# Value products ahead of a score tile behind a tanh, tanhs kept out of the last product steps, and a reordered tail in a fused attention and GEGLU block

## The chip, the cores and the metric

The kernel runs on one core of one Trainium2 chip. The metric is the device time of one execution in microseconds (us). The kernel before takes 1223.26 us, the median of 3 runs (1223.11 to 1223.34). Five engines work side by side: TensorE (PE, with its weight loads as PEld), VectorE (DVE), ScalarE (ACT), GpSimd (POOL) and SyncE (SP, which issues the DMAs).

## What is computed

A transformer block in bfloat16 on x of shape 1 x 2048 x 512, with 32 heads of 16 and a feed-forward width of 1792:

```python
q, k, v = split(layernorm(x) @ wqkv)
scores = einsum("bhqd,bhkd->bhqk", q, k) * Dh ** -0.5
h = x + merge(einsum("bhqk,bhkd->bhqd", softmax(scores), v)) @ wo
n = layernorm(h)
out = h + (gelu(n @ w_gate) * (n @ w_up)) @ w_down
```

The gelu is the tanh form. The scores are 32 x 2048 x 2048 values, each computed twice by this kernel: once for the row maximum, once (transposed) for the exp.

## The kernel before

**Units and ticks.** The queries are cut into 8 groups of 256, the heads into 8 slots of 4. A unit is one group and one slot (later ones: one half group and two slots); there are 64. The main loop (L1642) counts ticks, 16 to a unit. In each tick a first pass works on one unit and a second pass on the unit 24 ticks behind it:

- First pass: two matmuls (L883, `p1_pair`) write two 128 x 512 score tiles, and one reduction on DVE (L898) takes the row maxima of both. One tick of each of 14 units (JOINT) is saved by a difference trick on DVE (L895), with an `item_diff` that computes a difference beforehand.
- Second pass: two score tiles, transposed (L974, `p2_tile`), of which each gets its own exp on ACT (L1003) into a ring of 34 probability tiles.

Each score tile takes one of eight PSUM banks: four serve the first pass as a ring of two pairs, four (4 to 7) the second pass, handed out by `Banks` in the order in which they come free. A tile waits for the exp that last read its bank.

**The dense stream.** All other TensorE work is cut into pieces of about half a tick: generator functions that yield after some matmuls (`Dense`, L540). It holds one of the four banks while an item runs. Per tick one piece is issued, behind the two score tiles; without one, filler matmuls (L1618, `dummy`) take its place. The items are

- `item_pv` (L1006): the value products of one unit, probabilities times values, in four steps at ticks 15, 16, 17 and 18 of its second pass, which are ticks 7, 8, 9 and 10 of a unit by the loop's count. Behind the last step ACT copies the result out (OB, L727).
- the projections, the output projection (`item_oproj`, L1188), gate and up products of the feed-forward part (L1378, and L1323 in its half-group form), and down products (L1422).

**Gelu.** In the main stage the gelu is a polynomial on POOL (L1303 to L1305), a tanh on ACT (L1293) and two products on POOL (L1301, L1302), then a product with the up half (L1414 or L1359). When the tanh is recorded is decided by `later` in `gelu_chain` (L1285): it defers itself tick by tick while a model of ACT's backlog (`act_lag`) is too high or ticks are "tight".

**Order.** `Plan` records each engine's instructions in program order and derives the semaphore waits. The waits of a tick's first two matmuls and of its first score tile are gathered on the first of them (`group_begin`, `group_end`). Engines run their lists strictly in order. `deferred` calls run at the end of a tick, so what `later` records stands on ACT behind both exps of its tick.

**The end.** After the last first-pass tick, the second pass goes on alone: four tiles (two pairs) each even tick, one exp for each pair (L991), DVE takes over copies, and the dense stream fills PE. On an even tick `alone` keeps the cost of the dense piece, and on the odd tick behind it at least FILL_2 - alone is filled (L1737). There the last group's first half goes through `item_oprojA`, `item_hnA` (L1241), which transposes the normalized rows, and the raw gate and up products (GA, UA).

**The tail** (`tail_b`, L1549) computes the last half group: gelu of GA (L1517), GUT = GA * UA in four parts (`raw_mult`, L1521; part 0 on POOL, 1 to 3 on DVE), the output projection of the last rows (L1461 to L1567), their normalization (L1570 to L1577), transposes (`tail_hnT`, L1500) and copies (L1505, L1507), the seed of the last sums (`end_h`, L1541), gate, up and down products of the last 128 rows (L1323, L1546), while the down products of the rows before them (`down_mm`, L1422) are placed in between. `fill(n)` issues dense pieces, or fillers, worth n.

Of the kernel before, what the change touches and what calls it, by code (L numbers as in the profile page):

```python
# [215 lines left out]
NFC = F // 128  # L216
# [15 lines left out]
FILL_2 = 5  # L232
FILL_A = 2
# [15 lines left out]
def bass_sequential_preLN__mha_block__geglu_ffn__prompt_kernel(nc, A_x, A_wqkv, A_wo, B_x, B_w_gate, B_w_up, B_w_down, out):  # L249
    dbg = None  # L250
    with ExitStack() as es:
# [99 lines left out]
        GL = NG - 1  # L351
# [188 lines left out]
        class Dense:  # L540
            def __init__(self):
                self.prio = []
                self.ready = []
                self.extra = []
                self.gen = None
                self.under = None
                self.bank = None
                self.banks = [7, 3, 4, 5]
                self.rr = 0
                self.pause = 0  # L550
                self.single = False
                self.done = 0
                self.now = 0
# [6 lines left out]
            def _start(self, item):  # L560
                genfn, a, est, nb = item
                self.cur = genfn
                if self.single:
                    self.bank = banks.take()
                else:
                    self.bank = self.banks[self.rr % len(self.banks)]
                    self.rr += 1
                self.gen = genfn(self.bank, *a)
# [137 lines left out]

        act_lag = [0.0]
        def act_more(cost):
            act_lag[0] += cost
# [296 lines left out]
        def item_pv(b, ui, ps=(0, 1, 2, 3)):  # L1006
# [3 lines left out]
            for p in ps:  # L1010
                while not force[0] and dense.now < P2_START + 16 * ui + pt_t[p]:
                    yield ("wait", 1)
                for m in (2 * p, 2 * p + 1):
                    n, c0, s_ = (2, 0, slot) if ui < UB else (4, 128 * (m // 4), slot + m // 4)
                    qn = 512 // n
                    for i in range(n):
                        kt = 2 * m + i if ui < UB else 4 * (m % 4) + i
                        for g in range(4):
                            pi = pt_of[(ui, m, g)]
                            P.op("pe", lambda e, g=g, kt=kt, pi=pi, i=i, s_=s_, c0=c0, qn=qn: e.matmul(pbank[32 * g:32 * g + 17, b, c0:c0 + qn], VA[:, kt, 4 * s_ + g, :],  # L1020
                                                                                                      PTt(pi)[:, qn * i:qn * i + qn], start=(kt == 0), stop=(kt == NT - 1), tile_position=(0, 32 * g)),
                                 reads=[("V", kt), "VA_ones", ("PT", pi)], writes=[("pb", b)], sig=(g == 3 and i == n - 1))
                    for g in range(4):
                        pt_busy.discard(pt_of.pop((ui, m, g)))
                if p != ps[-1]:
                    yield 2
# [214 lines left out]
        def item_hnA(b):  # L1241
# [5 lines left out]
            defer(1, add_raw)  # L1247
            return 1
            yield
# [30 lines left out]
        def gelu_chain(par, dE, w=512):  # L1280
# [4 lines left out]
            def later(n):  # L1285
                if not force[0] and tight():
                    defer(1, lambda: later(n))
                    return
                if not force[0] and (act_lag[0] + (0.48 if dense.gen is not None and dense.cur in (item_gate, item_up, item_gate_h, item_up_h) else 0) > LAG_TH + SLOPE * n or poly_end[par] > TICK * dense.now + POLY):
                    defer(1, lambda: later(n + 1))  # L1290
                    return
                act_more(0.54 if w == 512 else 0.32)
                P.op("act", lambda e: e.activation(out=ts_, in_=ts_, func=ACT.Tanh, scale=GC), reads=[("th", par)], writes=[("th", par)])  # L1293
                defer(1, second)
# [254 lines left out]
        def tail_b():  # L1549
# [10 lines left out]
            while not a_done[0]:  # L1560
# [3 lines left out]
            in_bank(tail_onT)  # L1564
            raw_mult(1, "dve")
            fill(2)
# [8 lines left out]
            P.op("pool", lambda e: e.tensor_tensor(out=rstd2[:, tt], in0=rstd2[:, tt], in1=nhalf[:, 0:1], op=ALU.pow), reads=[("rstd2", t1), "nhalf"], writes=[("rstd2", t1)])  # L1575
            raw_mult(2, "dve")
            P.op("dve", lambda e: e.tensor_scalar(out=hn_sb[:, 1, :], in0=g_h(GL, 1), scalar1=mv2[:, t1, 0:1], scalar2=rstd2[:, tt], op0=ALU.subtract, op1=ALU.mult),  # L1577
                 reads=[("h", 1, 1), ("mv2", t1), ("rstd2", t1)], writes=[("OH", 1)])
            down_h(0, GL, 0)
            for fc in range(8):  # L1580
                down_mm(0, GL, 0, fc)
            fill(FILL_A)
            tail_hnT(2, (0, 1), "act")
            tail_hnT(3, (2, 3), "dve")
            raw_mult(3, "dve")
            for fc in chunks(2):
                down_mm(0, GL, 0, fc)
            while dense.busy():
# [5 lines left out]
            for t in range(NTL):  # L1594
                tail_gate(gb[2 * t % 5], t)
                tail_up(gb[(2 * t + 1) % 5], t)
                if t == 0:
                    for fc in chunks(3):
                        down_mm(0, GL, 0, fc)
# [42 lines left out]
        while True:  # L1642
# [37 lines left out]
            else:  # L1680
                t1 = p1_pair(tick // 16, tick % 16, gp1) if p1_ok else []
                if doubles[0]:
                    p1_next.append(p1_pair((tick + 1) // 16, (tick + 1) % 16, 1 - gp1))
            t2l = [next_tile()] if p2_ok and p1_ok else []
            P.group_end("pe")
            if p2_ok and p1_ok:
                behind[0] -= 1
                t2l.append(next_tile())
                if more:
# [36 lines left out]
            else:  # L1726
                cost = dense.piece()
                if cost and not p2_started:
# [63 lines left out]
```

## Time and profile before

| | |
|---|---|
| median of the runs | 1223.26 us |
| the profiled execution | 1223.57 us |
| its span, first to last instruction | 1221.5 us |
| granted TensorE clock | 1.000 |
| busy: PE, DVE, ACT, POOL | 1130.1, 1181.4, 1190.9, 840.0 us |
| reductions (L898) | 996, 1134.8 us busy |
| exps (L1003) | 2000, of 710 to 719 ns on average |
| tanhs (L1293) | 50, 42.9 us busy |
| value product matmuls (L1020) | 126.0, 51.2 and 41.8 us in three groups |
| fillers (L1618) | 771, 235.7 us busy |

Busy time is the time in which at least one instruction of an engine is under way. Consecutive instructions on ACT and DVE overlap at their ends, so a row's mean duration is longer than the distance from one start to the next. Rows of the timeline give the start, the duration, engine, line, operation, out<-in with shapes, and a count when like instructions are merged; in square brackets stands the idle time before, with what ended it. In the rows of `waits` stand the total, the number of waits, and the longest.

### The profile page before, as it was taken

The numbers are of one execution on the slowest core, as the hardware profiler recorded it, in microseconds if no ns is written. First come the engines' busy times: TensorE is split into PE (matmuls) and PEld (weight loads), VectorE is DVE, ScalarE is ACT, GpSimd is POOL, SyncE is SP. The second block draws the span as 40 slices with busy tenths as digits, with TensorE's granted clock in tenths as the row PEclk, the third lists the DMA queues.
The fourth block names the chain that finished last, engine by engine and source line by source line (L and its number), as shares of the span: only waits on it lengthen the run. The fifth ranks groups of instructions, "written<-read, shape, count | busy, mean of one in ns | idle before, by whom it ended". The sixth has DMA issues, their size and how long they took to land.

```text
span 1221.5 us, 36085 instructions
## 1 busy us (share of the span) xinstructions
PE 1130.1 (93%) x14842; PEld 476.2 (39%) x14842; DVE 1181.4 (97%) x1125; ACT 1190.9 (97%) x2422; POOL 840.0 (69%) x1772
## 2 busy tenths in 40 slices
PE   7999998899999999999999999999999999999998
PEld 3233332233333333333332333333334455554556
DVE  8999999999999999999999999999999999999973
ACT  7899999999999999999999999999999999999995
POOL 7567684756776586756868487774777687856771
PEclk9999999999999999999999999999999999999999
DMA  5111104300010000110001000100001100010000
GB/s 153 28 33 28 29 24 136 92 8 11 8 28 21 12 11 8 25 23 12 11 22 15 23 8 10 25 21 15 8 8 29 26 18 16 9 27 15 18 17 18
DMA packets 69651, 32.02 MB, mean 26 GB/s; under 512 B 54768, under 2 KB 68464, under 8 KB 69488
## 3 DMA queue, kind: packets, MB, share of 16 engines
q1 hardware_dynamic: 69488, 29.71, 10.0%
q8 instruction: 118, 1.93, 0.6%
q14 instruction: 45, 0.37, 0.1%
HBM read 11.80 MB, written 2.10 MB: 11 GB/s over the span
## 4 chain that ended last, share of the span: by engine, by line
ACT 55%; DVE 34%; PE 9%; issue 1%; POOL 0%; POOLq 0%; DVEq 0%
DVE PM L898 34%; ACT PTM L1003 31%; ACT PTG L1003 10%; ACT PTE L1003 5%; PE pbank L1422 2%; ACT th_sb L1293 2%; ACT g_sb L727 2%; ACT u_sb L727 2%; PE pbank L974 1%; PE pbank L1323 1%; PE pbank L883 1%; ACT OB L727 1%; PE pbank L456 1%; PE pbank L1618 1%; DVE OA L895 1%
## 5 line engine op out<-in xcount | busy, mean ns | idle before, releaser
L898 DVE TENSOR_REDUCE PM<-pbank 128x2 f32<-128x1024 f32 x996 | 1134.8, 1213 | 8.5 <-PE pbank L974 3.8
L1003 ACT ACTIVATE PTM<-pbank 128x512 bf16<-128x512 f32 x1357 | 733.4, 718 | 4.1 <-PE pbank L974 0.6
L974 PE MATMUL pbank<-QT,KT 32*128 32x256 bf16 (+1 forms) x5120 | 506.0, 250 | 14.4 <-ACT PTM L1003 7.9
L883 PE MATMUL pbank<-KT,QT 32*128 32x512 bf16 x2020 | 388.5, 384 | 24.9 <-DVE PM L898 10.2
L1618 PE MATMUL pbank<-ones_bf,ident 128*128 128x512 bf16 x771 | 235.7, 384 | 29.2 <-ACT PTM L1003 4.7
L883 PEld LDWEIGHTS pbank<-KT,QT 32*128 32x128 bf16 x2020 | 97.4, 91 | 350.8 <-DVE PM L898 130.8
L974 PEld LDWEIGHTS pbank<-QT,KT 32*128 32x128 bf16 x5120 | 205.5, 92 | 69.3 <-ACT PTM L1003 40.1
L1003 ACT ACTIVATE PTG<-pbank 128x512 bf16<-128x512 f32 x407 | 225.0, 710 | 0.8 <-PE pbank L974 0.4
L1003 ACT ACTIVATE PTE<-pbank 128x512 bf16<-128x512 f32 x236 | 140.2, 719 | 0.8 <-PE pbank L974 0.5
L1020 PE MATMUL pbank<-PTM,VA 128*17 128x256 bf16 (+1 forms) x3470 | 126.0, 252 | 1.8 <-ACT PTM L991 0.4
L1061 POOL TENSOR_TENSOR LINV<-OBT,negone 128x8 f32<-128x8 bf16 x63 | 105.1, 1669 | 5.7 <-DMA OBT<-OB 5.4
L1618 PEld LDWEIGHTS pbank<-ones_bf,ident 128*128 128x128 bf16 x771 | 45.1, 97 | 132.1 <-ACT PTM L1003 83.8
L1303 POOL TENSOR_TENSOR th_sb<-g_sb 128x512 f32<-128x512 f32 (+1 forms) x50 | 51.2, 1023 | 62.9 <-ACT g_sb L727 62.9
L1020 PEld LDWEIGHTS pbank<-PTM,VA 128*17 128x17 bf16 x3470 | 67.0, 90 | 40.5 <-issue 21.7
L1302 POOL TENSOR_TENSOR th_sb<-th_sb,g_sb 128x512 f32<-128x512 f32 (+1 forms) x50 | 62.4, 1249 | 4.0
L953 POOL TENSOR_TENSOR QT<-QT,STG 128x256 bf16<-128x256 bf16 x64 | 42.8, 668 | 31.3 <-DMA STG<-ST 30.7
L1305 POOL TENSOR_TENSOR th_sb<-th_sb,g_sb 128x512 f32<-128x512 f32 (+1 forms) x50 | 62.3, 1246 | 1.7
L1301 POOL TENSOR_SCALAR th_sb<-th_sb 128x512 f32<-128x512 f32 (+1 forms) x50 | 30.5, 611 | 40.9 <-ACT th_sb L1293 40.8
L1422 PE MATMUL pbank<-wd_sb,GUT 128*128 128x512 bf16 x210 | 57.8, 382 | 0.9 <-POOL GUT L1521 0.3
L798 POOL TENSOR_SCALAR QT<-QKS,qmask 128x512 bf16<-128x512 bf16 x30 | 46.9, 1569 | 13.4 <-ACT QKS L727 12.7
L1378 PE MATMUL pbank<-hnT_l,wg_sb 128*128 128x256 bf16 x336 | 51.2, 275 | 3.3 <-ACT PTM L1003 0.7
L1414 POOL TENSOR_TENSOR GUT<-th_sb,u_sb 128x512 bf16<-128x512 f32 x42 | 53.3, 1268 | 1.3
(197 smaller groups left out, 1210.2 us busy)
## 6 DMA issues: line engine op xcount, KB each, us to landing
QKS<-QKS SPq DMA_DIRECT2D x27, 112.0 KB, 2.1
x_sb<-in_A_x_dram SPq DMA_DIRECT2D x4, 512.0 KB, 5.7
xres<-in_A_x_dram SPq DMA_DIRECT2D x16, 128.0 KB, 2.3
out_dram<-out_sb SPq DMA_DIRECT2D x15, 128.0 KB, 1.7
wg_sb<-in_B_w_gate_dram SPq DMA_DIRECT2D x4, 448.0 KB, 4.2
wu_sb<-in_B_w_up_dram SPq DMA_DIRECT2D x4, 448.0 KB, 3.9
wd_sb<-in_B_w_down_dram SPq DMA_DIRECT2D x3, 512.0 KB, 4.4
STG<-ST SPq DMA_TRANSPOSE x64, 2.3
```

What stands on the lines that cost most here:

```text
L727: P.op("act", lambda e: e.activation(out=o_ap, in_=i_ap, func=ACT.Copy, **kw), reads=reads, writes=writes, extra_deps=extra)
L883: P.op("pe", lambda e, g=g, b=b: e.matmul(pbank[:, b, :], QT[32 * g:32 * g + 32, c, slot, 128 * qt:128 * qt + 128], KT[32 * g:32 * g + 32, ...
L898: P.op("dve", lambda e: e.tensor_reduce(out=PM[:, par, qt, kc, g:g + 2], in_=pbank[:, b:b + 2, :], axis=AX.X, op=ALU.max), reads=[("pb", b ...
L974: P.op("pe", lambda e, kt=kt, i=i: e.matmul(pbank[:, b, qn * i:qn * i + qn], KT[32 * g:32 * g + 32, slot, 128 * kt:128 * kt + 128], QT[32 ...
L1003: P.op("act", lambda e, b=b, pi=pi: e.activation(out=PTt(pi), in_=pbank[:, b, :], func=ACT.Exp), reads=[("pb", b)], writes=[("PT", pi)], e ...
L1020: P.op("pe", lambda e, g=g, kt=kt, pi=pi, i=i, s_=s_, c0=c0, qn=qn: e.matmul(pbank[32 * g:32 * g + 17, b, c0:c0 + qn], VA[:, kt, 4 * s_ + ...
L1061: P.op("pool", lambda e: e.tensor_tensor(out=li, in0=o4[:, :, :, 16], in1=negone[:, 0:4 * nq].rearrange("p (q h) -> p q h", q=nq), op=ALU. ...
L1302: o(1.27, lambda e: e.tensor_tensor(out=ts_, in0=ts_, in1=gs, op=ALU.mult), [("th", par), ("g", par)])], then=done)
L1305: o(1.27, lambda e: e.tensor_tensor(out=ts_, in0=ts_, in1=gs, op=ALU.mult), [("th", par), ("g", par)])], then=poly_done)
L1414: P.op("pool", lambda e: e.tensor_tensor(out=o_ap, in0=shp(ts_), in1=shp(us), op=ALU.mult), reads=[("th", par), ("u", par)], writes=o_keys ...
L1422: P.op("pe", lambda e: e.matmul(pbank[:, b, :], GUT[:, fc, 128 * k:128 * k + 128], wd_sb[:, fc, :], start=first, stop=last), reads=[("GUT" ...
L1618: P.op("pe", lambda e: e.matmul(pbank[:, b, :], ident[:], ones_bf[:, 0:512], start=True, stop=True), reads=["ident", "ones_bf"], writes=[( ...
```

## The change

Four things:

1. `dense.plain` is set while `item_pv` stands behind its first or second step. In the main loop, in a tick exactly two behind the one that recorded a tanh (`th_step`), with `dense.plain` set and no third tile, the dense piece (the second or third step of the value products) is issued between the two score tiles instead of behind them.
2. `later` doesn't record a tanh in ticks 9 and 10 of a unit while the value products are the running item; it tries again a tick later.
3. `item_hnA` returns FILL_2 (5) as its cost instead of 1, so that the odd tick behind it is not filled.
4. In the tail, GUT parts 1 and 2 are computed one place later on DVE (part 1 behind the statistics, part 2 behind the copies of the transposes), the FILL_A pieces come ahead of the seed `down_h` instead of behind eight down products, and down products 8 to 11, which stood behind the transposes, are issued with 12 and 13 behind the first gate and up products.

```diff
@@ Dense._start
                 self.cur = genfn
+                self.plain = False
@@ item_pv
+                dense.plain = p != ps[-1] and p + 1 != ps[-1]
                 if p != ps[-1]:
                     yield 2
@@ item_hnA
-            return 1
+            return FILL_2
@@ gelu_chain, later
-                if not force[0] and tight():
+                if not force[0] and (tight() or dense.gen is not None and dense.cur is item_pv and dense.now % 16 in (9, 10)):
                     defer(1, lambda: later(n))
                     return
...
                 act_more(0.54 if w == 512 else 0.32)
+                th_step[0] = dense.now
@@ tail_b
             in_bank(tail_onT)
-            raw_mult(1, "dve")
             fill(2)
...
-            raw_mult(2, "dve")
+            raw_mult(1, "dve")
             P.op("dve", lambda e: e.tensor_scalar(out=hn_sb[:, 1, :], ...
+            fill(FILL_A)
             down_h(0, GL, 0)
             for fc in range(8):
                 down_mm(0, GL, 0, fc)
-            fill(FILL_A)
             tail_hnT(2, (0, 1), "act")
             tail_hnT(3, (2, 3), "dve")
+            raw_mult(2, "dve")
             raw_mult(3, "dve")
-            for fc in chunks(2):
-                down_mm(0, GL, 0, fc)
...
                 if t == 0:
-                    for fc in chunks(3):
+                    for fc in range(8, NFC):
                         down_mm(0, GL, 0, fc)
@@ main loop
+            mid = 0
             t2l = [next_tile()] if p2_ok and p1_ok else []
             P.group_end("pe")
             if p2_ok and p1_ok:
                 behind[0] -= 1
+                if dense.plain and tick - th_step[0] == 2 and not more:
+                    mid = dense.piece()
                 t2l.append(next_tile())
...
-                cost = dense.piece()
+                cost = mid or dense.piece()
```

More of the change, by code (lines that the diff above doesn't have):

```diff
@@ L562, in _start @@
                 self.cur = genfn
+                self.plain = False
                 if self.single:
@@ L707, in bass_sequential_preLN__mha_block__geglu_ffn__prompt_kernel @@
         act_lag = [0.0]
+        th_step = [-9]
         def act_more(cost):
```

## Prediction

> **What bounds the kernel now.** I read the page first, then busy time by stage, then the waits, then the timeline at the places that the change touches.
>
> ```profile
> ACT 55%; DVE 34%; PE 9%; issue 1%; POOL 0%; POOLq 0%; DVEq 0%
> ...
> L898 DVE TENSOR_REDUCE PM<-pbank 128x2 f32<-128x1024 f32 x996 | 1134.8, 1213 | 8.5 <-PE pbank L974 3.8
> ```
>
> The chain that ended last runs over ACT and DVE. The 996 reductions of L898 cover 1134.8 us of a span of 1221.5 and DVE idles only 8.5 us before them.
>
> ```profile
> 100.00:1177.00 1077.00, 1002.44 (x13361) 416.30 (x13360) 1070.59 (x983) 1071.28 (x2201) 754.24 (x1601) 1.00 0.10 23
> 1177.00:1201.40 24.40, 22.23 (x579) 15.55 (x579) 9.58 (x21) 23.40 (x28) 14.08 (x23) 1.00 0.07 19
> 1201.40:1221.50 20.10, 16.50 (x190) 12.12 (x190) 7.77 (x17) 8.09 (x15) 2.21 (x2) 1.00 0.07 21
> ```
>
> The columns are length, then PE, PEld, DVE, ACT, POOL busy, and the granted clock. In the main stage (100 to 1177) DVE idles 1077.00 - 1070.59 = 6.4 us: that is what better order can win there, and a little more (below). In the end, where no reductions are left (1177 to 1201.4), ACT is full. In the tail PE is the busiest, in a chain of short dependent steps.
>
> ```profile
> PE pbank L974 <- ACT PTM L1003: 7.9, 26, 0.6
> ...
> DVE PM L898 <- PE pbank L974: 3.8, 16, 0.3
> ```
>
> PE waits 26 times, 7.9 us in all, ahead of a score tile for an exp to free its bank, and 16 times DVE then visibly waits for PE. Where is that?
>
> ```profile
> 460.40 0.92 ACT L1293 ACTIVATE th_sb<-th_sb 128x512 f32<-128x512 f32 x1
> ...
> 460.92 0.89 ACT L1003 ACTIVATE PTM<-pbank 128x512 bf16<-128x512 f32 x1
> ...
> 461.25 0.39 PE L974 MATMUL pbank<-QT,KT 32*128 32x256 bf16 x2
> ...
> 461.39 2.40 ACT L1003 ACTIVATE PTE<-pbank 128x512 bf16<-128x512 f32 x4
> ...
> 461.86 0.39 PE L974 MATMUL pbank<-QT,KT 32*128 32x256 bf16 x2 [0.23 <-ACT PTM L1003]
> ...
> 462.18 0.61 PE L1020 MATMUL pbank<-PTM,VA 128*17 128x256 bf16 x16
> ...
> 462.73 0.39 PE L883 MATMUL pbank<-KT,QT 32*128 32x512 bf16 x2
> ```
>
> The reader is to see one tick. A tanh (L1293) stands on ACT two ticks back, so the exp that frees the second tile's bank is late; PE idles 0.23 us in front of that tile, and the value products (L1020), which wait for nothing, stand behind it. The next pair of L883 so comes late, and DVE after it:
>
> ```profile
> 460.70 7.28 DVE L898 TENSOR_REDUCE PM<-pbank 128x2 f32<-128x1024 f32 x6
> ```
>
> ```profile
> 475.82 4.61 DVE L898 TENSOR_REDUCE PM<-pbank 128x2 f32<-128x1024 f32 x4
> 480.63 1.23 DVE L898 TENSOR_REDUCE PM<-pbank 128x2 f32<-128x1024 f32 x1 [0.21 <-PE pbank L974]
> ```
>
> Four undisturbed reductions take 4.61 us: with 1.21 for the last, one starts every 1.13 us. Six would take 6.87; the first row's six took 7.28, 0.41 lost in two stalls. A stall costs its idle time and 0.08 us more, because neighbours otherwise overlap by 1.21 - 1.13.
>
> **The change part by part.** The order of instructions shows: the value products go ahead of the second tile in 27 ticks, each two ticks behind a tanh; five tanhs of the main stage and one in the end move two ticks (four exps and an OB copy) later; four filler matmuls of L1618 go; the tail is reordered. DMAs, POOL's and SP's order are the same. So ACT's and DVE's work is the same, and only waits can change.
>
> *1. The 27 ticks.* There are two kinds and one odd tick. In 20 the wait in front of tile 2 is 0.23 us, as above. The products start 0.32 us after a tile's start and hold PE 0.55 us (462.18 - 461.86, 462.73 - 462.18). Put behind tile 1 they run from 461.57 to 462.12, so tile 2 starts at 462.12 instead of 461.86: 0.26 us later. The next group needs no products before it, only the bank of the exp at 461.39; that exp is 0.47 us behind the one at 460.92, which released tile 2 at 461.86, so the group can start at about 462.36 instead of 462.73. DVE then has its pair 0.37 earlier and its stall here (0.11 idle, 0.19 lost) goes. But ACT is the second limit: its four exps took 2.40 us, where three spacings of 0.48 and a last one of 0.6 make 2.04, so it starved 0.37 there. Moved, it starves about 0.25 us for tile 2 instead and then no more: ACT is only 0.12 us ahead. Since DVE stalls a second time in the same row of six, two ticks on, ACT is still close to holding it up, and I count ACT's gain, not DVE's: 0.11 us in the 18 of these ticks that have a stall behind them, 2.0 us. The ends: nothing (ACT gives all back), and DVE's whole loss, about 3.1 us over them (0.02 to 0.27 idle a time in the timeline, and 0.08).
>
> ```profile
> 478.40 0.39 PE L974 MATMUL pbank<-QT,KT 32*128 32x256 bf16 x2
> ...
> 479.33 0.39 PE L974 MATMUL pbank<-QT,KT 32*128 32x256 bf16 x2 [0.55 <-ACT PTM L1003]
> ...
> 479.65 0.40 PE L1020 MATMUL pbank<-PTG,VA 128*17 128x256 bf16 x8
> ...
> 480.20 0.39 PE L883 MATMUL pbank<-KT,QT 32*128 32x512 bf16 x2
> ```
>
> In six ticks (this is one, the last has the row below) PE waits 0.55 us. Here the products end at 478.40 + 0.87 = 479.27, before the bank is free at 479.33: they are hidden whole. The next group starts 0.48 behind, at 479.81 instead of 480.20, and its reduction can start at 480.24, before DVE is free at 480.35. Each gives 0.21 + 0.08 = 0.29 us: 6 x 0.29 = 1.7 us (at worst half, if one tick later PE is late again; at best 2.6, if a smaller stall some ten ticks on goes too).
>
> ```profile
> 1114.37 1.23 DVE L898 TENSOR_REDUCE PM<-pbank 128x2 f32<-128x1024 f32 x1 [0.21 <-PE pbank L974]
> ```
>
> The Trainium skill (TensorEngine Tiling (Array Packing), Tiling Modes, Key Properties) says that a change of tiling mode drains TensorE. By it the second tile pays the drain behind the products; two changes a tick remain two, and the 0.55 us from the products to the next row-tiled pair holds one already, so the sum stays, but a dearer drain is what rival 3 would need.
>
> *2. No tanh in the last two steps.*
>
> ```profile
> 498.84 0.87 ACT L1293 ACTIVATE th_sb<-th_sb 128x512 f32<-128x512 f32 x1
> ...
> 500.32 0.65 ACT L727 ACTIVATE OB<-pbank 128x256 bf16<-128x256 f32 x1
> ```
>
> ```profile
> 501.71 2.36 DVE L898 TENSOR_REDUCE PM<-pbank 128x2 f32<-128x1024 f32 x2 [0.28 <-PE pbank L974]
> ```
>
> ```profile
> 934.80 2.35 DVE L898 TENSOR_REDUCE PM<-pbank 128x2 f32<-128x1024 f32 x2 [0.17 <-PE pbank L974]
> ```
>
> A second tanh falls into the last steps of the products and is followed by the OB copy: DVE stalls 0.28 us four times, 0.17 the fifth time. Behind OB the products' bank is free again, so a tile waits for an exp four back instead of three, and a tanh there is covered by the extra bank. Queued behind the moved tanh on ACT are the exps of two ticks; PE waits for them. I take all of it: 4 x 0.36 + 0.25 = 1.7 us; the other end is nothing, if the tanh stalls as much in its new place. POOL gets its input two ticks, 2.26 us, later; I cost that at nothing, since its order and PE's are the same and the down products that read its result come many ticks on. If they waited, it would be up to 2.26 us at each place.
>
> *3. The end (FILL_2).*
>
> ```profile
> 1180.03 2.91 ACT L991 ACTIVATE PTM<-pbank 128x1024 bf16<-128x1024 f32 x3
> ...
> 1181.70 0.40 PE L1244 MATMUL pbank<-ident,OnT 128*128 128x128 bf16 x4 [1.04 <-DVE OnT L1235]
> 1181.94 1.03 PE L1618 MATMUL pbank<-ones_bf,ident 128*128 128x512 bf16 x4
> ...
> 1183.38 2.94 ACT L991 ACTIVATE PTM<-pbank 128x1024 bf16<-128x1024 f32 x3 [0.44 <-PE pbank L974]
> ```
>
> Four fillers run while ACT runs dry: 2.91 us for three pairs is one per 0.91, so the next was due at 1182.75 and came at 1183.38, 0.63 us late. Without the fillers the tiles start at 1181.95, written by 1182.4. ACT is full from there to 1201.4, so 0.6 us go (ends: 0.3, as other waits follow; 0.9, all four fillers).
>
> *4. The tail.*
>
> ```profile
> 1203.98 1.34 DVE L1521 TENSOR_TENSOR GUT<-GA,UA 128x512 bf16<-128x512 f32 x1 [0.22 <-ACT GA L1517]
> 1205.24 0.69 DVE L1570 BATCH_NORM_STATS2 stats<-pbank 128x6 f32<-128x512 f32 x1
> ...
> 1206.25 0.68 DVE L1521 TENSOR_TENSOR GUT<-GA,UA 128x512 bf16<-128x512 f32 x1
> 1207.45 0.41 DVE L1577 TENSOR_SCALAR OnT<-xres,mv,rstd 128x512 bf16<-128x512 bf16 x1 [0.52 <-POOL rstd L1575]
> 1208.36 0.29 DVE L1507 COPY hnT_l<-pbank 128x256 bf16<-128x256 bf16 x1 [0.49 <-PE pbank L1500]
> ```
>
> ```profile
> 1203.97 0.38 PE L1567 MATMUL pbank<-wo_sb,OnT 128*128 128x512 bf16 x1
> ...
> 1204.83 2.33 PE L1422 MATMUL pbank<-wd_sb,GUT 128*128 128x512 bf16 x10 [0.26 <-POOL GUT L1521]
> ...
> 1207.92 0.40 PE L1500 MATMUL pbank<-ident,OnT 128*128 128x128 bf16 x4 [0.55 <-DVE OnT L1577]
> 1208.16 1.03 PE L1422 MATMUL pbank<-wd_sb,GUT 128*128 128x512 bf16 x4
> ...
> 1211.46 1.06 PE L1323 MATMUL pbank<-hnT_l,wg_sb 128*128 128x128 bf16 x16
> ```
>
> The statistics (L1570) read what L1567 wrote by 1204.35, but stand behind a 1.34 us product. With that product moved they start at 1204.40: 0.84 us earlier, and L1577 at 1206.61. The product takes the place of the next, 0.68 us from 1205.41 to 1206.09, and its four L1422 (0.22 us each) end at 1207.0, just when the transposes (L1500) can start, 1207.08: 0.84 gained. Then the four L1422 that stood in front of the gate are gone, and PE instead waits for the copies: L1507 ended 0.73 us behind L1500's start, the two seeds of L1541 fill 0.4 of it, so 0.38 us are lost. The L1422 come back behind the up product, and from 1211.46 on all is as before: 0.84 - 0.38 = 0.46, say 0.5 us. The ends: 0.84, and -0.1 if the moved product again takes 1.34.
>
> **Sum:** 2.0 + 1.7 + 1.7 + 0.6 + 0.5 = 6.5 us. The profiled execution took 1223.57 (span 1221.5 and 2.07 around it), so 1217.1; the median of the runs is 0.3 lower, so **1216.8**.
>
> **The rivals.** (1) *ACT gives back.* ACT's exps are nearly back to back, and a DVE that isn't held up only finds ACT later. Then the 20 ticks give 0.5, the six 0.9, the tanhs 0.9, end and tail 1.1: 3.4 us, 1219.9. For it: DVE and ACT both idle under 0.6% of the main stage. Against: ACT starved 0.37 us in these very ticks.
> (2) *The stalls only move*, one tick on, where again a tile waits ahead of products, and the tanhs stall at their new place; the change doesn't do what it says, and end and tail alone give 1.1: 1222.2.
> (3) *The products hold up the second tile.* It decides at the place 461.86: tile 2 starts 0.87 behind tile 1 by the rows; at 1.0 ACT gains nothing, and each 0.1 beyond costs 20 x 0.1 = 2 us, which ACT cannot recover. At 1.4 this costs 8 us, less 4.5 from the other parts: 1226.8, slower.
> (4) *The clock falls* with the fillers gone. The granted clock is 1.00 in all three stages, and PE already idles 1.04 us before L1244 at that. Half the clock over the 11 us of matmuls from 1208 would add up to 11: 1228. The Trainium skill (TensorE: Matmul & The Clock Gate, Why this matters for your kernels) sets the limit at idle gaps of about 3 us; the trace agrees as far as it goes, since 1.04 us cost no clock.
>
> **How the numbers follow.** The forecast 0.72, rival 1 0.16, rival 2 0.07, rival 3 0.04, rival 4 0.01. What a measurement can tell from no change is 0.2%, 2.4 us: faster means under 1220.8, so 0.72 and 0.16 give 0.88; same 0.07; slower 0.05. Low end: DVE's whole loss in the 27 ticks (3.1 and 2.6), tanhs 1.7, end and tail 0.9 and 0.8, 9.1 us: 1214.2, of which I take 1214.6. High end: rival 1, 1220.0.
>
> **What would show it.** In the profile after: PE's waits before L974 (7.9 us, 26 times) should fall below 3 us; the 16 visible stalls of DVE to about three or four, main-stage idle of 6.4 us to about 2 to 3; no idle of 0.44 us at the first exp pair behind the transposes; L1570 behind L1567 within 0.1 us; a wait of about 0.4 us before the first gate product. Wrong would be: exps in the 20 ticks that start later than now relative to the reductions, and new DVE stalls two or three ticks behind the place.

## The result, and the profile after

The changed kernel takes 1220.11 us (median of 8 runs; 1219.59 to 1220.41) beside 1223.11 us of the kernel before (8 runs; the 1223.26 above is of three of them): a ratio of 0.9971, 95% interval 0.9963 to 0.998. It is 3.0 us faster, where 6.5 were forecast. The direction was right and the size about half; the time lies 0.1 us beyond the slow end of the range that the prediction gave, 1220.0. Line numbers of the new kernel are 3 to 5 higher in the functions of interest: L883 is now L886, L974 is L977, L1003 is L1006, L1020 is L1023, L898 is L901, L1293 is L1298.

The page after, first the chain that ended last, then the costliest group on DVE:

```profile
ACT 50%; DVE 40%; PE 8%; issue 2%; DMA 1%; POOL 1%
...
L901 DVE TENSOR_REDUCE PM<-pbank 128x2 f32<-128x1024 f32 x996 | 1134.2, 1215 | 5.7 <-PE pbank L977 1.8
```

Busy time by stage (length, then PE, PEld, DVE, ACT, POOL busy and the granted clock). End and tail are cut at the same events as before; the main stage starts at 100 us in both. PE's lower count is mostly of matmul records that are missing from this trace: the fillers' weight loads are 767, four fewer than before, their matmul records 659 beside 771.

```profile
100.00:1174.09 1074.09, 979.12 (x13229) 417.53 (x13359) 1069.97 (x982) 1068.93 (x2200) 751.96 (x1601) 1.00 0.09 23
1174.09:1197.81 23.72, 21.06 (x572) 15.25 (x575) 9.55 (x21) 23.23 (x28) 14.08 (x23) 1.00 0.08 20
1197.81:1217.50 19.69, 16.46 (x188) 12.09 (x190) 7.12 (x17) 7.98 (x15) 2.20 (x2) 1.00 0.07 21
```

The waits that the prediction wanted gone are gone. PE's, ahead of a score tile for an exp (7.9 us, 26 times before):

```profile
PE pbank L977 <- ACT PTM L1006: 0.3, 1, 0.3
```

and DVE's for PE (3.8 us, 16 times before):

```profile
DVE PM L901 <- PE pbank L977: 1.8, 7, 0.4
```

PE's wait fell to 0.3 us, further than forecast, and yet DVE's idle time in the main stage fell only from 6.4 to 1074.09 - 1069.97 = 4.1 us. So taking PE's wait away did not buy the time behind it. The difference of the two traces, 3.98 us from the first instruction to the last, splits into 0.44 at the start-up (which scatters by up to 1.1 us over the kernels below, all with the same start), 2.50 in the main stage (from the start of the 31st reduction to that of the last), 0.64 in the end and 0.41 in the tail. End and tail came as forecast; in the main stage 5.4 were.

**Where the gain of the moved products went: a tick of the first kind.** The row of the prediction had four exps in 2.40 us behind a tanh, and took ACT to starve 0.37 there. Here are PE, then DVE, of the new kernel at the same tick:

```profile
460.24 0.39 PE L977 MATMUL pbank<-QT,KT 32*128 32x256 bf16 x2
460.55 0.61 PE L1023 MATMUL pbank<-PTM,VA 128*17 128x256 bf16 x16
461.10 0.39 PE L977 MATMUL pbank<-QT,KT 32*128 32x256 bf16 x2
461.34 0.39 PE L886 MATMUL pbank<-KT,QT 32*128 32x512 bf16 x2
...
464.16 0.39 PE L886 MATMUL pbank<-KT,QT 32*128 32x512 bf16 x2 [0.26 <-ACT PTG L1006]
```

```profile
458.56 5.79 DVE L901 TENSOR_REDUCE PM<-pbank 128x2 f32<-128x1024 f32 x5
464.59 1.23 DVE L901 TENSOR_REDUCE PM<-pbank 128x2 f32<-128x1024 f32 x1 [0.24 <-PE pbank L977]
```

The products stand between the tiles, the second tile starts 0.86 us behind the first (0.87 was worked out), the stall right behind is gone: five reductions run without a stall. Two ticks on DVE stalls 0.24 us, where it stalled 0.11 before. ACT tells why. Before:

```profile
460.40 0.92 ACT L1293 ACTIVATE th_sb<-th_sb 128x512 f32<-128x512 f32 x1
460.92 0.89 ACT L1003 ACTIVATE PTM<-pbank 128x512 bf16<-128x512 f32 x1
461.39 2.40 ACT L1003 ACTIVATE PTE<-pbank 128x512 bf16<-128x512 f32 x4
...
464.17 0.39 ACT L727 ACTIVATE OB<-pbank 128x256 bf16<-128x256 f32 x1
```

and after:

```profile
459.39 0.92 ACT L1298 ACTIVATE th_sb<-th_sb 128x512 f32<-128x512 f32 x1
459.91 0.89 ACT L1006 ACTIVATE PTM<-pbank 128x512 bf16<-128x512 f32 x1
460.38 2.37 ACT L1006 ACTIVATE PTE<-pbank 128x512 bf16<-128x512 f32 x4
...
462.97 0.55 ACT L730 ACTIVATE OB<-pbank 128x256 bf16<-128x256 f32 x1
```

Read these by their ends. Before, the first exp ends at 460.92 + 0.89 = 461.81 and the four at 461.39 + 2.40 = 463.79: 1.98 us for four, 0.495 each. After it is 460.80 and 462.75: 1.95. From the tanh's start to the end of the OB copy it is 4.16 us before and 4.13 after. The exp that had to wait for PE started 0.37 us late and yet ended only 0.03 late: one that starts while its predecessor is still under way takes up to 0.93 us, one that starts late 0.60, and the ends keep their distance. Four at 0.49 make 1.96, so ACT was starved of no more than 0.02 to 0.03 us here, and 0.03 us is what the move gained.

**A tick of the second kind** looks alike on ACT, before and after:

```profile
477.87 0.92 ACT L1293 ACTIVATE th_sb<-th_sb 128x512 f32<-128x512 f32 x1
478.39 2.88 ACT L1003 ACTIVATE PTM<-pbank 128x512 bf16<-128x512 f32 x5
```

```profile
476.83 0.92 ACT L1298 ACTIVATE th_sb<-th_sb 128x512 f32<-128x512 f32 x1
477.35 2.85 ACT L1006 ACTIVATE PTM<-pbank 128x512 bf16<-128x512 f32 x5
```

Five exps end 2.48 us behind the tanh's end before, 2.45 after. DVE's 0.29 us came at once and went again in steps (0.14, 0.10 and 0.04 us), one and six to eight ticks on, at the next tiles that waited for ACT.

**The account of one period.** The pattern of tanhs repeats every 126 ticks. With ACT's instructions in order of their ends, an exp, or a copy of 512 columns, ends 0.49 us behind the one before when ACT is fed, a tanh 0.51, an OB copy 0.28; what is more than that is starvation. (Two short instructions of about 0.09 us that read out a sum are counted for themselves.) In the kernel before, from 404.5 to 516.4 us, with four of the 27 places and the late tanh in it (the one of the last product steps, which part 2 moves), no step exceeds this by more than 0.06 us. Apart from these small steps, all starvation of the period, 2.0 us, lies in the 32 us behind it. In 112 of the period's 144 us ACT alone sets the time, and a stall of DVE there is only its shadow. From the end of the first to the end of the last, the same 256 exps take (a late transfer is a DMA that landed late, see below)

| kernel | us for the period | starvation in steps of over 0.055 us | in smaller steps |
|---|---|---|---|
| before | 143.87 | 2.00 | 0.17 |
| part 1 alone (e1) | 144.06 | 2.17, of it 0.24 by a late transfer | 0.18 |
| part 2 alone (e2) | 143.50 | 1.59 | 0.21 |
| after without part 1 (e9) | 143.51 | 1.59 | 0.22 |
| after | 143.38 | 1.58 | 0.10 |

So behind part 2, part 1 is worth the 0.12 us of small steps in a period (0.22 to 0.10), and with four of its 27 places to a period that makes 0.8 us in all. Alone, it takes nothing off them (0.17 and 0.18).

### The profile page after: what moved, and what is told of

It reads as the page before. It is cut to its first block, busy times and chain, and to the rows that moved or that the text cites. A ratio compares the mean times of both kernels' runs of the same rounds, so it can differ in the third digit from the quotient of the medians.

```text
span 1217.5 us, 35931 instructions
## 1 busy us (share of the span) xinstructions
PE 1103.6 (91%) x14692; PEld 476.7 (39%) x14838; DVE 1180.5 (97%) x1125; ACT 1188.8 (98%) x2422; POOL 837.9 (69%) x1772
## 4 chain that ended last, share of the span: by engine, by line
ACT 50%; DVE 40%; PE 8%; issue 2%; DMA 1%; POOL 1%
DVE PM L901 38%; ACT PTM L1006 28%; ACT PTG L1006 9%; ACT PTE L1006 5%; PE pbank L1427 2%; ACT g_sb L730 2%; ACT u_sb L730 2%; ACT th_sb L1298 1%; PE pbank L977 1%; PE pbank L1328 1%; PE pbank L886 1%; ACT OB L730 1%; DVE OA L898 1%; ACT OA L1115 1%; PE pbank L1621 1%
## 5 line engine op out<-in xcount | busy, mean ns | idle before, releaser
L901 DVE TENSOR_REDUCE PM<-pbank 128x2 f32<-128x1024 f32 x996 | 1134.2, 1215 | 5.7 <-PE pbank L977 1.8
L1006 ACT ACTIVATE PTM<-pbank 128x512 bf16<-128x512 f32 x1357 | 736.3, 737 | 3.5 <-PE pbank L977 0.6
L977 PE MATMUL pbank<-QT,KT 32*128 32x256 bf16 (+1 forms) x5120 | 513.6, 250 | 8.4 <-ACT PTG L1006 0.4
L886 PE MATMUL pbank<-KT,QT 32*128 32x512 bf16 x2020 | 388.5, 384 | 23.9 <-DVE PM L901 8.6
L1621 PE MATMUL pbank<-ones_bf,ident 128*128 128x512 bf16 x659 | 208.3, 384 | 51.8 <-ACT PTM L1006 21.7
L977 PEld LDWEIGHTS pbank<-QT,KT 32*128 32x128 bf16 x5120 | 207.6, 92 | 70.4 <-ACT PTM L1006 37.7
L886 PEld LDWEIGHTS pbank<-KT,QT 32*128 32x128 bf16 x2020 | 96.6, 91 | 341.9 <-DVE PM L901 126.7
L1006 ACT ACTIVATE PTG<-pbank 128x512 bf16<-128x512 f32 x407 | 227.0, 728 | 0.8 <-PE pbank L977 0.4
L1006 ACT ACTIVATE PTE<-pbank 128x512 bf16<-128x512 f32 x236 | 141.7, 735 | 0.8 <-PE pbank L977 0.5
L1023 PE MATMUL pbank<-PTM,VA 128*17 128x256 bf16 (+1 forms) x3470 | 126.0, 252 | 2.0 <-ACT PTM L994 0.4
L1023 PEld LDWEIGHTS pbank<-PTM,VA 128*17 128x17 bf16 x3470 | 67.0, 90 | 40.9 <-issue 21.7
L1427 PE MATMUL pbank<-wd_sb,GUT 128*128 128x512 bf16 x191 | 54.5, 382 | 3.4 <-ACT PTM L1006 0.8
```

What stands on the lines that cost most here:

```text
L886: P.op("pe", lambda e, g=g, b=b: e.matmul(pbank[:, b, :], QT[32 * g:32 * g + 32, c, slot, 128 * qt:128 * qt + 128], KT[32 * g:32 * g + 32, ...
L901: P.op("dve", lambda e: e.tensor_reduce(out=PM[:, par, qt, kc, g:g + 2], in_=pbank[:, b:b + 2, :], axis=AX.X, op=ALU.max), reads=[("pb", b ...
L977: P.op("pe", lambda e, kt=kt, i=i: e.matmul(pbank[:, b, qn * i:qn * i + qn], KT[32 * g:32 * g + 32, slot, 128 * kt:128 * kt + 128], QT[32 ...
L1006: P.op("act", lambda e, b=b, pi=pi: e.activation(out=PTt(pi), in_=pbank[:, b, :], func=ACT.Exp), reads=[("pb", b)], writes=[("PT", pi)], e ...
L1427: P.op("pe", lambda e: e.matmul(pbank[:, b, :], GUT[:, fc, 128 * k:128 * k + 128], wd_sb[:, fc, :], start=first, stop=last), reads=[("GUT" ...
L1621: P.op("pe", lambda e: e.matmul(pbank[:, b, :], ident[:], ones_bf[:, 0:512], start=True, stop=True), reads=["ident", "ones_bf"], writes=[( ...
```

## The experiments

Main stage below is the time from the start of the 31st reduction to that of the last, end that from there to the last exp's end, tail that from there to the end of the last copy on ACT (the span goes on for 1.97 us behind it in before and after), each from the profiled execution. Each ratio is to runs of the kernel before in the same batch, whose medians were 1223.11 us for the result, 1223.48 for e1 to e4, 1223.91 for e5, e6, e9 and e10, and 1223.65 for e11 to e14; medians of different batches are not compared. Equal instructions gave 1121.79, 1121.99 and 1122.41 us for the main stage (before, e3, e4), so differences under 0.6 us there need the place as well. The scatter lies at a few places. In single executions a transposing DMA, on which a first score tile depends by way of POOL's L953, takes up to 2.1 us more than its usual 2.3; and around 970 and 1076 us PE sometimes pauses for 0.2 us and more, with no wait that the trace names.

| kernel | median us | ratio to before, 95% interval | main | end | tail |
|---|---|---|---|---|---|
| before | 1223.11 | | 1121.79 | 25.58 | 18.18 |
| after | 1220.11 | 0.9971 (0.9963 to 0.998) | 1119.29 | 24.94 | 17.77 |
| e1_mid | 1223.31 | 0.9997 (0.9988 to 1.0006) | 1122.02 | 25.58 | 18.18 |
| e2_tanh | 1222.05 | 0.9988 (0.9979 to 0.9997) | 1120.03 | 25.58 | 18.17 |
| e3_end | 1223.31 | 0.9999 (0.999 to 1.0008) | 1121.99 | 25.21 | 18.17 |
| e4_tail | 1223.56 | 1.0 (0.9992 to 1.0009) | 1122.41 | 25.58 | 17.76 |
| e9_nomid | 1221.14 | 0.9977 (0.9968 to 0.9987) | 1120.51 | 24.94 | 17.77 |
| e5_mid23 | 1220.69 | 0.9973 (0.9962 to 0.9983) | 1120.16 | 24.95 | 17.77 |
| e6_midall | 1223.46 | 0.9995 (0.9986 to 1.0004) | 1123.61 | 24.95 | 17.77 |
| e10_mid23last | 1224.49 | 1.0003 (0.9994 to 1.0012) | 1124.39 | 24.94 | 17.77 |
| e11_nomid_shortdiff | 1217.37 | 0.995 (0.9937 to 0.9962) | 1116.97 | 24.94 | 17.77 |
| e12_mid_shortdiff | 1216.29 | 0.9942 (0.9929 to 0.9954) | 1115.96 | 24.94 | 17.77 |
| e13_nomid_shorttanh | 1211.7 | 0.9903 (0.9888 to 0.9918) | 1111.32 | 24.92 | 17.76 |
| e14_mid_shorttanh | 1212.31 | 0.9908 (0.9895 to 0.9922) | 1111.71 | 24.93 | 17.77 |

### The four parts alone

**e1_mid**, the kernel before with

```diff
+                if dense.plain and tick - th_step[0] == 2 and not more:
+                    mid = dense.piece()
```

(and the lines of the diff above that set `plain`, `th_step` and `cost`).

> The kernel before with part 1 alone: the value products ahead of the second tile in the 27 ticks, nothing else. Theory (most of it comes back): the stalls right behind the 27 ticks go, but the wait for a late exp stands in front of the second tile of the next tick, with products behind it, so ACT and DVE lose most of the gain one to ten ticks later: 0.8 us faster (0.4 to 1.2). The forecast, with each gain kept: 3.7 us faster. Rival (the whole main-stage gain is the tanhs' and the products give nothing): within 0.2 us.

Next to nothing was gained: 0.2 us by the medians, inside the interval. The main stage is 0.23 us longer, with 0.24 lost at a late transfer and about 0.3 around 1076 us, so that 0.3 at most can have been won. The rival is the nearest, and the theory's 0.8 is not there. The stalls behind the places vanish here as in the kernel after. What they gave is lost at the last in the row, the stall of the late tanh, which grew from 0.28 to 0.40 us:

```profile
501.80 2.36 DVE L901 TENSOR_REDUCE PM<-pbank 128x2 f32<-128x1024 f32 x2 [0.40 <-PE pbank L977]
```

**e2_tanh**, the kernel before with

```diff
-                if not force[0] and tight():
+                if not force[0] and (tight() or dense.gen is not None and dense.cur is item_pv and dense.now % 16 in (9, 10)):
```

> The kernel before with part 2 alone: no tanh in the last two steps of the value products. Theory, and the forecast: five moved tanhs keep 0.36 us each, the fifth a little less, 1.7 us faster (1.4 to 2.0). Rival (a tanh stalls as much at its new place, and only together with the moved products does it pay): under 0.5 us.

The main stage is 1.76 us shorter, in four steps of 0.36 and one of 0.34, each kept to the end. Theory and forecast held; the medians (1.4 us, interval 0.4 to 2.6) agree.

**e3_end**, the kernel before with

```diff
-            return 1
+            return FILL_2
```

> The kernel before with part 3 alone: no fillers behind the transposes of the last group's first half. Theory, and the forecast: the first exp pair behind the transposes starts without its 0.44 us idle, and ACT is full from there, 0.6 us faster. Rival (a later wait takes the place): under 0.2 us.

0.37 us in the end by the trace, too little for the medians. ACT then meets a tanh whose input isn't ready:

```profile
1187.66 0.42 ACT L1293 ACTIVATE th_sb<-th_sb 128x256 f32<-128x256 f32 x1 [0.39 <-POOL th_sb L1305]
```

In the kernel after, part 2 has moved this tanh behind two more instructions of L991 (L994 there), the wait is covered, and the end gains 0.64: a small debt that two parts pay together.

**e4_tail**, the kernel before with part 4 alone (the last hunks of the diff above, of `tail_b`).

> The kernel before with part 4 alone: GUT parts 1 and 2 one place later on DVE, the pieces ahead of the seed, four down products behind the first gate and up products. Theory, and the forecast: 0.84 us gained at the statistics, 0.38 lost in front of the gate, 0.5 us faster. Rival (the moved product takes 1.34 us again beside POOL's product, or the gate waits longer): 0.1 us slower to 0.1 us faster.

0.42 us in the tail by the trace; the median, whose interval is wider than that, shows nothing.

### Part 1 on top of the others, and more of it

**e9_nomid**, the kernel after with part 1 taken out again.

> The changed kernel without part 1: products behind the second tile everywhere; tanh rule, end and tail as changed. From the trace of part 2 alone the main stage should be 1.76 us shorter than before, and end and tail as after. Theory (part 1 pays only where no tanh stands a few ticks behind it, since ACT's backlog gives the rest back): 0.7 us slower than the changed kernel, of which all in the main stage. Rival (part 1 pays nothing, as when it was put in alone): as the changed kernel, within 0.3 us. The forecast (part 1 is worth 3.7): 3.7 us slower.

The ratio is 0.0006 above that of the kernel after, 0.7 us, as the theory of this run had it, but the two intervals overlap; the traces have to decide. The main stages differ by 1.22 us, of which 0.3 are a late transfer (DVE idles 0.71 us there without part 1 and 0.36 with it). What is left is seen on DVE as one stall of 0.10 us at the last place of a period (498.64 us here), which part 1 removes seven times for good; in e1 the late tanh's stall took it back. So part 1, worth next to nothing alone, is worth 0.7 to 0.9 us behind part 2: what it passes on no longer ends in the late tanh's stall.

**e5_mid23**, the kernel after with

```diff
-                if dense.plain and tick - th_step[0] == 2 and not more:
+                if dense.plain and tick - th_step[0] in (2, 3) and not more:
```

> The changed kernel, with the products ahead of the second tile also three ticks behind a tanh: six more places, 33 in all, each one tick behind a place of the second kind. Theory (the wait only moved to the second tile of the next tick, with products behind it): the new stall of about 0.05 us one tick on goes, with its 0.08, so 0.13 at six places, 0.8 us faster than the changed kernel. Rival (ACT's backlog is the limit, wherever PE puts the products): within 0.2 us of the changed kernel, the loss coming back at the next stall some nine ticks on.

Next to no gain. The theory of this run, that the wait had only moved to PE's next tile, fell. The small stall one tick on went, 0.15 us each time, and DVE stalled some six ticks behind the place instead, by 0.12 more than in the kernel after: six reductions that took 6.87 us undisturbed take

```profile
482.43 7.11 DVE L901 TENSOR_REDUCE PM<-pbank 128x2 f32<-128x1024 f32 x6
```

The six places together gave 0.2 us, the rival's bound. The 0.87 us by which its main stage is longer than that of the kernel after were lost at the places that scatter (0.56 at a late transfer, 0.15 around 970 and 0.44 around 1076 us).

**e6_midall**, the kernel after with the condition on the tanh left out.

> The changed kernel, with the products ahead of the second tile in every second and third step of the value products, 124 places instead of 27, tanh or not. In the new places no exp is late, so the second tile comes later than it need, about 0.87 us behind the first. Theory (ACT has slack there and takes it up): within 0.5 us of the changed kernel. Rival (the products hold up the second tile, ACT loses about 0.2 us at each and cannot recover it): slower by 5 us or more.

In this trace 3.55 of the 4.32 us lost in the main stage go at one place. There the transfer lands 4.4 us after its issue, and behind it the clock falls (columns as above, clock third from the right):

```profile
840.00:855.00 15.00, 13.65 (x148) 5.91 (x142) 15.00 (x15) 15.00 (x33) 8.81 (x18) 1.00 0.06 11
855.00:858.00 3.00, 1.27 (x33) 0.64 (x26) 1.51 (x2) 2.11 (x5) 1.87 (x3) 1.00 0.00 0
858.00:864.50 6.50, 6.50 (x70) 2.36 (x67) 5.22 (x5) 4.94 (x11) 3.68 (x7) 0.51 0.05 10
```

```profile
856.13 0.67 POOL L956 TENSOR_TENSOR QT<-QT,STG 128x256 bf16<-128x256 bf16 x1 [2.50 <-DMA STG<-ST]
```

Up to this place 0.84 us had been lost, behind it the losses and the gains at places that scatter even out. So the 97 more places cost little, about 0.01 us each, and far less than the rival's 0.2, but the sum is above the theory's 0.5. And none of the eleven runs was under 1221.88, while this trace without the one place would give about 1220.4, so the other runs lost time that this trace doesn't explain; this stays open.

**e10_mid23last**, the kernel after with

```diff
-                dense.plain = p != ps[-1] and p + 1 != ps[-1]
+                dense.plain = p != ps[-1]
...
-                if dense.plain and tick - th_step[0] == 2 and not more:
+                if dense.plain and tick - th_step[0] in (2, 3) and not more:
```

> The changed kernel, with the products ahead of the second tile two and three ticks behind a tanh, and in the last step too: 58 places (6, 27 and 25 in steps two, three and four). Theory (each wait moves to the next tick's second tile until the products are over): 0.8 us from the second kind as with 33 places, and about 0.1 us at each of some 20 of the first kind, up to 2.8 us faster than the changed kernel in all. Rival (ACT's backlog is the limit, wherever PE puts the products): within 0.3 us of the changed kernel.

Both missed: it is 3.9 us slower than the kernel after by the ratios, 5.1 in the main stage. ACT now starves 0.17 us at 464.5 and at 500.5, inside the stretch where it had been full, and each time it is the OB copy that starts late:

```profile
462.17 1.89 ACT L1006 ACTIVATE PTE<-pbank 128x512 bf16<-128x512 f32 x3
464.12 0.38 ACT L730 ACTIVATE OB<-pbank 128x256 bf16<-128x256 f32 x1
464.40 0.59 ACT L1006 ACTIVATE PTE<-pbank 128x512 bf16<-128x512 f32 x1
```

The edit does more than move products. The OB copy is recorded with the last step, so with this step between the tiles it stands ahead of both exps of its tick in ACT's list, where it stood behind them. It waits for the products, which end at 464.07, while the tile of the first of these exps was written by 463.52. So this run tests the copy's place on ACT, and not whether the products hold up the second tile.

### Taking work off ACT

**e11_nomid_shortdiff** and **e12_mid_shortdiff**, without and with part 1, the copies of the difference items cut:

```diff
+            nc_ = 512 if ui == min(JOINT) else 32
-            P.op("act", lambda e: e.activation(out=RB[:, g, :], in_=pbank[:, b, :], func=ACT.Relu), ...
+            P.op("act", lambda e: e.activation(out=RB[:, g, 0:nc_], in_=pbank[:, b, 0:nc_], func=ACT.Relu), ...
```

> The changed kernel without part 1, and with the copy of the difference items (two on ACT per joint unit) cut to 32 of 512 columns in all joint units but the first, so the differences are not all computed. It takes about 0.4 us off ACT two to nine ticks behind some of the places. It is the yardstick for the next run. Both theories: within 0.5 us of the same kernel with whole copies, a little faster where these copies now make DVE wait.

> As the run before, with part 1 (the value products ahead of the second tile in 27 ticks); the copies cut in the same way. Theory (part 1's gain is given back where ACT, still behind from the tanh, gets the next copy): at the five places followed by a difference item the 0.16 us given back two ticks on stays, so part 1 is now worth about 1.5 us against the run before, instead of about 0.7. Rival (it is the bank held by the difference item, or PE's order, not ACT's time): about 0.7, and the stalls of 0.23 us two ticks on remain.

The yardstick itself was off: it is 3.5 us shorter in the main stage, where 0.5 was the most expected. The stalls of the second kind (0.21 us) vanish by it, without any move of products. Part 1 is then worth 1.0 us (1116.97 - 1115.96; 1.1 by the medians), of which about 0.2 is a late transfer that the run without it met at 423 us, and not 1.5; and DVE's stalls of 0.23 us two ticks behind places of the first kind remain:

```profile
463.76 2.35 DVE L901 TENSOR_REDUCE PM<-pbank 128x2 f32<-128x1024 f32 x2 [0.23 <-PE pbank L977]
```

My guess at which ACT instruction stands in the way was wrong, and the rival was right that it isn't this copy. ACT's rows with part 1 show what it is:

```profile
461.67 0.75 ACT L1006 ACTIVATE PTG<-pbank 128x512 bf16<-128x512 f32 x1
462.15 0.55 ACT L730 ACTIVATE OB<-pbank 128x256 bf16<-128x256 f32 x1
462.41 1.27 ACT L1006 ACTIVATE PTG<-pbank 128x512 bf16<-128x512 f32 x2
463.37 0.40 ACT L1116 ACTIVATE OA<-pbank 128x32 f32<-128x32 f32 x1
```

The exp that frees the bank is the first of the two at 462.41; the cut copy (463.37) stands behind it, the tanh and the OB copy (462.15) ahead of it.

**e13_nomid_shorttanh** and **e14_mid_shorttanh**, without and with part 1, every tanh of the main stage cut:

```diff
-                P.op("act", lambda e: e.activation(out=ts_, in_=ts_, func=ACT.Tanh, scale=GC), ...
+                P.op("act", lambda e: e.activation(out=ts_[:, 0:32], in_=ts_[:, 0:32], func=ACT.Tanh, scale=GC), ...
```

> The changed kernel without part 1, and with every main-stage tanh cut to 32 of 512 columns, so the gelu is not computed whole. Theory (the stalls of DVE are ACT's backlog behind a tanh): they vanish without any move of products, and the main stage gets 3 to 5 us shorter than with whole tanhs. Rival (the stalls come from the products' place on PE): at most 1 us shorter.

> As the run before, with part 1 (the value products ahead of the second tile in 27 ticks); tanhs cut in the same way. Theory (part 1 does nothing but pass ACT's backlog on): with the backlog gone it is worth nothing, within 0.4 us of the run before in the main stage, or a little slower, since the products then hold up the second tile for nothing. Rival (part 1 takes a delay out of PE's order as such): again about 0.7 us faster than the run before.

Without the tanhs' time the main stage is 9.2 us shorter than with them (1120.51 to 1111.32), where 3 to 5 were expected, and DVE's stalls behind second-pass tiles nearly vanish:

```profile
DVE PM L898 <- PE pbank L883: 1.5, 3, 0.8
DVE PM L898 <- PE pbank L974: 0.9, 2, 0.6
```

```profile
100.00:1165.05 1065.05, 961.21 (x13220) 411.08 (x13351) 1064.07 (x982) 1056.11 (x2199) 754.25 (x1601) 1.00 0.10 23
```

DVE idles 1.0 us in the main stage. Without this backlog part 1 costs 0.4 us instead of gaining (0.6 by the medians). The direction is the theory's in both runs, the size in the first only half of what was measured: the stalls are ACT's backlog, and part 1 can pass it on but hardly shorten it. The tanh is not its only part, since cutting other copies in e11 took 3.5 us off the main stage as well.

## Why the prediction was half right

*What bounds the kernel* was read one level too high. DVE's idle 6.4 us were taken as what better order can win. They were for the most part the shadow of ACT, which is full in 112 of the 144 us of the period worked out above, and order on PE can win there only what ACT starves.

*Step 1, the 27 ticks* (3.7 us forecast, 0.7 to 0.9 measured, next to nothing alone) is the step that failed. Its PE part was right to 0.01 us. Its sentence "ACT is the second limit: its four exps took 2.40 us, where three spacings of 0.48 and a last one of 0.6 make 2.04, so it starved 0.37 there" is wrong: 2.40 us is first start to last end, a sum in which the first exp's 0.9 us overlap with what stood before it. The 0.6 of the last is the length of an exp that starts late, while the first took 0.9. By ends the four took 1.98 us, and 0.03 at most was starved. For the six ticks of the second kind I left ACT out altogether and counted DVE's gain; the lower end that I gave ("at worst half, if one tick later PE is late again") was still too high. Rival 1, that ACT gives back, has the mechanism, and its time (1219.9) is the nearest; it was put aside with this same starvation ("Against: ACT starved 0.37 us in these very ticks"). But it cut the tanhs to a half as well, and the products to 1.4 of 3.7 us, while in fact the products gave a fifth and the tanhs all; that its time fits is in part luck.

*Step 2, the tanhs* (1.7 forecast, 1.76 measured) was right, and the account gives a reason that the prediction did not have. The late tanh's stall is the last one before ACT has caught up. Behind it DVE sets the time, and the starvation of 0.19 and 0.16 us at 516.6 and 517.7 goes with it. A gain is kept where the limit changes hands; seen from there, a stall further up was worth next to nothing.

*Step 3, the end* (0.6 forecast, 0.64 measured): ACT runs through, without the idle 0.44 us. That the size fits is luck in part. The prediction took ACT to be full from there on, and by itself part 3 gave only 0.37, because the next tanh then waits 0.39 us for its input (e3); only part 2 covers this wait, which the prediction had not worked out.

```profile
1177.09 7.58 ACT L994 ACTIVATE PTM<-pbank 128x1024 bf16<-128x1024 f32 x8
```

*Step 4, the tail* (0.5 forecast, 0.41 measured), in the rows of the kernel after:

```profile
1200.40 0.38 PE L1571 MATMUL pbank<-wo_sb,OnT 128*128 128x512 bf16 x1
...
1200.81 0.70 DVE L1574 BATCH_NORM_STATS2 stats<-pbank 128x6 f32<-128x512 f32 x1 [0.64 <-PE pbank L1571]
...
1201.83 0.68 DVE L1526 TENSOR_TENSOR GUT<-GA,UA 128x512 bf16<-128x512 f32 x1
...
1203.51 0.40 PE L1505 MATMUL pbank<-ident,OnT 128*128 128x128 bf16 x4
...
1204.27 0.28 PE L1546 MATMUL pbank<-xres,ident 128*128 128x256 bf16 x1 [0.25 <-ACT hnT_l L1510]
1204.39 1.06 PE L1328 MATMUL pbank<-hnT_l,wg_sb 128*128 128x128 bf16 x16
```

The statistics start 0.41 us behind the start of L1571, that is when its 0.38 us are over, where they stood 1.27 behind; the moved product takes 0.68; the transposes come 3.11 us behind L1571 instead of 3.95, the 0.84 worked out; and in front of the gate PE waits for the copies. The loss there and at the returning products is 0.84 - 0.41 = 0.43 us, 0.38 worked out.

*The other rivals.* The stalls did move (rival 2), but not those of the tanhs. The second tile was not held up (0.86 us behind the first, 1.0 the point of decision). The clock stayed at 1.00 in all three stages.

*The signs* named in the prediction show the error by themselves: PE's wait fell to 0.3 us and DVE's stalls from 16 to 7 instead of to three or four, and the new stalls "two or three ticks behind the place" that were to prove it wrong are there: 0.24 us where it was 0.11.

## What to carry to other kernels

Where instructions of an engine overlap, measure whether it is starved by the distance of their ends, never by starts or by a group's length. Before a stall is priced, look for the engine that is behind over a whole stretch: inside the stretch, removing other engines' waits only passes them on, and the time is won by taking work off that engine or by moving the last stall before it has caught up. Try each part alone and also missing from the whole, since part 1 was worth next to nothing in the one and 0.7 to 0.9 us in the other.

## What the runs showed of the hardware that was not expected

- An exp of 128x512 from PSUM takes 0.58 to 0.94 us by its record and, when ACT is fed, 0.49 us of ACT's time from end to end. A start that was 0.37 us late cost 0.03 us. The Trainium skill (ScalarE: Activation LUTs, What ACT_TABLE_LOAD costs) gives 186 ns + 0.833 ns per element for such an instruction without a pointer operand and 93 ns of overlap between neighbours; an estimate from it, 520 ns, is near the 0.49 and would have shown that four in 1.98 us leave no gap.
- PE idle for 1.73 us (e6, at 855.2 us) was followed by a granted clock of 0.51 for 6.5 us; idle for 1.04 and 1.11 us in the same trace was not. The Trainium skill (TensorE: Matmul & The Clock Gate, Why this matters for your kernels) puts the limit at gaps of about 3 us; here one of 1.73 came before the fall, with PE only 1.27 us busy in the 3 us from 855, so idle time around the gap may count with it. The length of a gap alone does not decide in these runs: in e2, e3 and e4 the clock was 0.50 for 3.4 us from about 23 us on, behind the same idle 1.11 us at 21 us that no fall follows in the other eleven traces. These three have the longest start-ups, 54.5 to 54.7 us to the 31st reduction beside 53.6 to 54.0. What decides stays open.
- The same small transposing DMA took 2.3 us from issue to landing in most cases and up to 4.4 in others. The clock's fall in e6 followed such a late landing, and much of the main stage's scatter between executions came from it.
